# Eight K loads cut into 112 rows and four transfers of four rows, and seven 126-row dk stores moved to other heads

## The chip, the cores and the metric

One core of one Trainium2 chip. The metric is the device time of one execution in microseconds (us), as the median of several runs.

## The reference, cut to what matters

```python
B, H, Sq, Sk, D = 2, 32, 1, 8192, 128          # bf16
def fwd(q, k, v):
    scores = einsum("bhqd,bhkd->bhqk", q, k) * D ** -0.5
    return einsum("bhqk,bhkd->bhqd", softmax(scores), v)
# outputs: fwd, and its gradients dq, dk, dv for a given grad_out
```

There are 64 heads. Each reads a K and a V matrix of 8192 x 128 bf16 (2,048 KB each) and writes a dK and a dV of the same size. That is 537 MB in all, against little arithmetic, so the kernel is a stream.

## The kernel before

A K or V matrix lies in SBUF as a tile of 128 partitions with 64 x 128 bf16 each: a *row* of 16 KB per partition. There are twelve such tiles. VectorE overwrites K and V with dK and dV, and the tile is stored and then filled again, six heads later. Loads are issued by SyncE (queue q1 of the profile), stores by GpSimd (q0). Both queues are served by the same 16 DMA engines: in the trace of the kernel before, the longest unbroken chain of packets, each starting 3 or 4 ns before the end of the last (426 packets, from 87 to 312 us), holds load rows of q1 and store rows of q0, in turn at 87% of its steps.

```python
SPREAD = range(5, 64, 9)
...
def by_rows(eng, dst, src, rows):
    p = 0
    for m in rows:
        pin(eng.dma_start(out=dst[p : p + m], in_=src[p : p + m], max_dma_last_dim=NT * D))
        p += m

def load(i, w, pieces=(NCH,)):                 # w = 0: K, w = 1: V
    h = heads[i]
    t = kvp.tile([P, NT, D], BF16, tag=f"kv{slot_of(i, w)}", name="kvt")
    h.tile[w] = t
    src = (v_v if w else k_v)[i]
    c = 0
    for m in pieces:
        n0, n1 = c * CH, (c + m) * CH
        pin(load_eng.dma_start(out=t[:, n0:n1, :], in_=src[:, n0:n1, :]))
        c += m
...
def outer(i, w, c, ends):                      # dK (w = 0) or dV, into the tile, and its store
    ...
    if w == 0 and i in SPREAD:
        by_rows(store_eng, dst, h.tile[w], (P - 2, 2))
    else:
        eng = load_eng if len(ends) > 1 else store_eng
        pin(eng.dma_start(out=dst[:, b0:b1, :], in_=h.tile[w][:, b0:b1, :]))
```

A normal load is one transfer of 128 rows, eight for each engine (eight 16 KB packets for each load in that chain). The dk stores of the seven heads in `SPREAD` go as 126 rows and 2 rows. The chain has 18 packets of 8 KB, or nine rows, of such a store, so 126 rows fill 14 engines, and most of the work is kept off the other two (4 and 5 by the prediction's reading of the trace). No profile shows an engine's number: the numbers in this document are my names for chains of packets.

## Time and profile before

| | before |
|---|---|
| time, median of 3 runs | 1288.12 us (1287.0 to 1288.25) |
| moved by DMA | 539.68 MB |
| TensorE busy | 88% of the span |
| ScalarE, VectorE busy | 76%, 73% |
| DMA busy | 90% or more in 39 of 40 slices |

The profile page of the kernel before opens with the span and the busy time of each engine (us, share, instructions), and further down counts the DMA packets:

```profile
span 1286.9 us, 42575 instructions
...
PE 1131.8 (88%) x19268; PEld 860.1 (67%) x19268; DVE 935.9 (73%) x2122; ACT 975.2 (76%) x641; POOL 75.1 (6%) x142
...
DMA packets 39986, 539.68 MB, mean 419 GB/s; under 512 B 5116, under 2 KB 5116, under 8 KB 6396
```

No compute engine is full over the whole run. 539.68 MB at a mean of 419 GB/s is the time. The prediction shows the DMA, queue and chain lines; they say that the DMA engines are the bound. This stretch of the middle of the kernel before (columns: stretch and length, busy us and instructions of TensorE, weight load, VectorE, ScalarE and GpSimd, TensorE clock, DMA share, GB/s) is the mark to compare with later:

```profile
120.00:160.00 40.00, 39.36 (x704) 30.41 (x703) 33.51 (x76) 35.40 (x24) 3.54 (x6) 1.00 1.01 427
```

In this early stretch TensorE is nearly full as well (39.36 of 40 us). Over the run it is not: it is 88% busy, and 91.6 us of the rest are waits for loads (below).

### The profile page before, as it was taken

How to read it: one execution, taken by the hardware profiler on the slowest of the kernel's cores; microseconds unless marked ns; L12 is line 12 of the kernel's file. 1: busy time of each engine (PE TensorE's matmuls, PEld its weight loads, DVE VectorE, ACT ScalarE, POOL GpSimd, SP SyncE). 2: the span in 40 equal slices, each digit the busy share in tenths (PEclk: the TensorE clock that was granted, in tenths of full speed). 3: DMA queues.
4: the chain of work that ended last, by engine and by line, in shares of the span. 5: the costliest groups of instructions: out<-in, count | busy, mean ns of one | idle time of the engine just before them, and what ended most of it. 6: DMA issues, size and time to landing. Idle time of an engine off the chain costs nothing.

```text
span 1286.9 us, 42575 instructions
## 1 busy us (share of the span) xinstructions
PE 1131.8 (88%) x19268; PEld 860.1 (67%) x19268; DVE 935.9 (73%) x2122; ACT 975.2 (76%) x641; POOL 75.1 (6%) x142
## 2 busy tenths in 40 slices
PE   6999999988899988989899988889898988988880
PEld 5777777766677666766666766667666666766650
DVE  2888888777687777767776876777767777777781
ACT  6888888877788777867777877778777777777750
POOL 0000000000000000000000000000000000000000
PEclk9999999999899999989899998999999999999985
DMA  9999999999999999999999999999999999999995
GB/s 388 424 425 427 427 427 427 426 427 428 428 426 427 428 427 426 416 429 427 427 427 429 427 427 427 427 424 424 426 427 428 426 427 424 427 428 428 424 392 216
DMA packets 39986, 539.68 MB, mean 419 GB/s; under 512 B 5116, under 2 KB 5116, under 8 KB 6396
## 3 DMA queue, kind: packets, MB, share of 16 engines
q1 hardware_dynamic: 20172, 272.70, 49.8%
q0 software_dynamic: 19632, 264.25, 48.7%
q8 instruction: 150, 2.46, 0.7%
q14 instruction: 32, 0.26, 0.0%
HBM read 268.47 MB, written 268.47 MB: 417 GB/s over the span
## 4 chain that ended last, share of the span: by engine, by line
DMA 38%; PE 26%; another core or an unknown queue 19%; DVE 10%; issue 4%; ACT 1%; SPq 1%; POOL 0%; POOLq 0%; DVEq 0%; ACTq 0%
DMA kvt<-in_v_dram 29%; PE tp L184 11%; PE acc L339 6%; DVE kvt L394 6%; DMA kvt<-in_k_dram 5%; DMA out_dram<-kvt 4%; PE dpw L195 3%; PE sw L195 3%; DVE sel L362 2%; ACT ev L186 1%; PE dpw L282 1%; SPq L98 1%; DVE sel L356 1%; DMA qd_nat<-in_q_dram 1%
## 5 line engine op out<-in xcount | busy, mean ns | idle before, releaser
L186 ACT COPY ev<-tp 128x2048 bf16<-128x2048 bf16 x512 | 954.4, 1865 | 266.1 <-PE tp L184 254.4
L184 PE MATMUL tp<-ident_bf,kvt 128*128 128x128 bf16 x8192 | 559.9, 223 | 91.6 <-DMA kvt<-in_v_dram 71.6
L394 DVE TENSOR_TENSOR kvt<-qb,pair 128x2048 bf16<-128x2048 bf16 x512 | 621.4, 1214 | 0.3
L184 PEld LDWEIGHTS <-kvt 128*128 128x128 bf16 x8192 | 490.5, 101 | 98.3 <-DMA kvt<-in_v_dram 75.1
L195 PEld LDWEIGHTS <-ev 128*128 128x128 bf16 x8192 | 243.1, 96 | 210.0 <-issue 152.5
L339 PE MATMUL acc<-kvt,dS_pad 128*64 128x512 bf16 x1024 | 169.2, 413 | 0.8 <-DVE dqT L379 0.8
L339 PE MATMUL acc<-kvt,E_pad 128*64 128x512 bf16 x1024 | 161.0, 395 | 0.0
L195 PE MATMUL dpw<-qdT,ev 128*128 128x1 bf16 x4096 | 140.8, 164 | 17.7 <-DVE qb L177 16.9
L362 DVE SCALAR_TENSOR_TENSOR sel<-acc,diag,sel 128x128 f32<-128x128 f32 x384 | 134.7, 351 | 13.6
L195 PE MATMUL sw<-qdT,ev 128*128 128x1 bf16 x4096 | 142.0, 164 | 1.2 <-ACT ev L186 1.2
L412 POOL DMA_DIRECT2D out_dram<-kvt x119 | 63.7, 536 | 1087.6 <-DVE kvt L394 922.1
L207 DVE TENSOR_REDUCE mp<-sw 128x1 f32<-128x64 f32 x64 | 14.4, 224 | 151.8 <-PE sw L195 151.8
L339 PEld LDWEIGHTS <-dS_pad 128*64 128x64 bf16 x1024 | 37.7, 111 | 24.7 <-issue 5.9
L247 DVE CAST E_pad<-E_f 128x64 bf16<-128x64 f32 x64 | 12.5, 195 | 55.4 <-ACT E_f L238 55.4
L339 PEld LDWEIGHTS <-E_pad 128*64 128x64 bf16 x1024 | 36.5, 109 | 21.4 <-issue 0.9
L376 PE MATMUL acc<-ones,sel 128*128 128x1 f32 x256 | 43.6, 239 | 6.2 <-DVE sel L362 6.2
L282 PE MATMUL dpw<-ld,ones 128*128 128x1 f32 x256 | 46.3, 250 | 0.1
L253 DVE CUSTOM_DVE_ANT_0 junk<-E_f,dpw 128x64 bf16<-128x64 f32 x64 | 14.1, 221 | 43.7 <-PE dpw L195 43.7
L376 PEld LDWEIGHTS acc<-ones,sel 128*128 128x128 f32 x256 | 39.3, 194 | 7.3 <-DVE sel L362 7.3
L356 DVE TENSOR_SCALAR sel<-acc,diag 128x128 f32<-128x128 f32 x128 | 44.1, 344 | 0.0
L177 DVE CAST qb<-dpw 128x128 bf16<-128x128 f32 x128 | 35.5, 277 | 6.2 <-PE dpw L168 6.2
L282 PEld LDWEIGHTS dpw<-ld,ones 128*128 128x128 f32 x256 | 38.2, 189 | 0.5 <-DVE ld L253 0.5
(44 smaller groups left out, 313.2 us busy)
## 6 DMA issues: line engine op xcount, KB each, us to landing
out_dram<-kvt POOLq DMA_DIRECT2D x119, 2048.0 KB, 66.9
kvt<-in_v_dram SPq DMA_DIRECT2D x64, 2048.0 KB, 20.9
kvt<-in_k_dram SPq DMA_DIRECT2D x63, 2048.0 KB, 20.9
out_dram<-kvt POOLq DMA_DIRECT2D x7, 2016.0 KB, 70.3
out_dram<-kvt SPq DMA_DIRECT2D x8, 512.0 KB, 24.0
kvt<-in_k_dram SPq DMA_DIRECT2D x2, 512.0 KB, 4.7
kvt<-in_k_dram SPq DMA_DIRECT2D x1, 1024.0 KB, 7.3
out_dram<-kvt POOLq DMA_DIRECT2D x7, 32.0 KB, 69.7
```

What stands on the lines that cost most here:

```text
L177: pin(nc.vector.tensor_copy(out=h.qb[w][:], in_=h.qbp))
L184: pin(nc.tensor.transpose(tp[:, t, :], src[:, c * CH + t, :], ident_bf[:]))
L186: pin(nc.scalar.copy(out=ev[:], in_=tp[:]))
L195: nc.tensor.matmul(dst[:, c * CH + t : c * CH + t + 1], lhsT=ev[:, t, :], rhs=qdT[:, w, i : i + 1], start=True, stop=True,)
L207: pin(nc.vector.reduce_max(out=h.mp[:], in_=h.s, axis=AX.X))
L282: nc.tensor.matmul(out, lhsT=ones[:].to_broadcast([P, P]), rhs=col, start=True, stop=True)
L339: nc.tensor.matmul(h.acc[w][g : g + CW, :], lhsT=wts[:, n0 : n0 + CW], rhs=rows[:, n0 : n0 + QT, :].rearrange("p n d -> p (n d)"), start=( ...
L356: nc.vector.tensor_scalar(out=h.sel[:], in0=block, scalar1=diag[:, 0:1], scalar2=None, op0=ALU.mult)
L362: nc.vector.scalar_tensor_tensor(out=h.sel[:], in0=block, scalar=diag[:, b : b + 1], in1=h.sel[:], op0=ALU.mult, op1=ALU.add,)
L376: nc.tensor.matmul(h.acc[w][:, 0:1], lhsT=h.sel[:], rhs=ones[:], start=True, stop=True)
L394: nc.vector.tensor_tensor(out=h.tile[w][:, n0 : n0 + CH, :].rearrange("p n (e t) -> p n e t", t=2), in0=h.qb[w][:] .rearrange("p (e t) -> ...
L412: pin(eng.dma_start(out=dst[:, b0:b1, :], in_=h.tile[w][:, b0:b1, :]))
```

## The change

Intent: engines 0 to 3 seemed to have less work than the others at the end of the kernel. In eight K loads, the change moves one row from each of engines 4 to 15 to engines 0 to 3: 112 rows over all 16 engines (seven each), then four transfers of four rows, each on four engines. The step of 4 in the row index picks, for each small transfer, rows that lie four partitions apart. The seven dk stores without engines 4 and 5 come every eight heads from head 4, in place of every nine from head 5.

```diff
-SPREAD = range(5, 64, 9)
+EXTRA = range(8, 64, 7)
+SPREAD = range(4, 56, 8)
...
         src = (v_v if w else k_v)[i]
+        if w == 0 and i in EXTRA:
+            m = P - 16
+            pin(load_eng.dma_start(out=t[:m], in_=src[:m]))
+            for j in range(4):
+                r = slice(m + j, P, 4)
+                pin(load_eng.dma_start(out=t[r], in_=src[r], max_dma_last_dim=NT * D))
+            return
         c = 0
```

## The prediction

14.6 us for 24 rows and 0.3 us for their small packets make 14.9, and 1,288.1 + 14.9 = 1,303, taken as 1,302.5. That engines 0 to 3 get 7 + 4 rows was an assumption.

> **What bounds the kernel now.** I read the page's forty slices first, then the queues, the chain of work that ended last, the DMA issues, the stretches of the last 67 us, and at last the single DMA packets.
>
> ```profile
> DMA  9999999999999999999999999999999999999995
> GB/s 388 424 425 427 427 427 427 426 427 428 428 426 427 428 427 426 416 429 427 427 427 429 427 427 427 427 424 424 426 427 428 426 427 424 427 428 428 424 392 216
> q1 hardware_dynamic: 20172, 272.70, 49.8%
> q0 software_dynamic: 19632, 264.25, 48.7%
> q8 instruction: 150, 2.46, 0.7%
> q14 instruction: 32, 0.26, 0.0%
> DMA 38%; PE 26%; another core or an unknown queue 19%; DVE 10%; issue 4%; ACT 1%; SPq 1%; POOL 0%; POOLq 0%; DVEq 0%; ACTq 0%
> out_dram<-kvt POOLq DMA_DIRECT2D x119, 2048.0 KB, 66.9
> kvt<-in_k_dram SPq DMA_DIRECT2D x63, 2048.0 KB, 20.9
> out_dram<-kvt POOLq DMA_DIRECT2D x7, 2016.0 KB, 70.3
> ```
>
> The 16 DMA engines are busy in every slice but the last, at some 427 GB/s. Loads (q1) and stores (q0) share them about evenly. A store needs 66.9 us to land while a head (two loads, two stores) takes about 1,287/64 = 20 us, so some six or seven stores always stand in line. TensorE is 88% busy, with waits for loads in it. The DMA engines are the bound, and what remains is how evenly they are loaded. The last 27 us show that they are not even:
>
> ```profile
> 1220.00:1240.00 20.00, 18.56 (x333) 14.45 (x332) 15.32 (x38) 16.35 (x13) 1.06 (x2) 1.00 1.00 402
> 1240.00:1260.00 20.00, 11.37 (x82) 5.55 (x80) 17.34 (x36) 1.86 (x1) 0.53 (x1) 0.60 0.96 393
> 1260.00:1287.00 27.00, 0.00 (x0) 0.00 (x0) 0.00 (x0) 0.00 (x0) 0.00 (x0) 0.50 0.43 177
> ```
>
> These are stretches with the busy time of TensorE, its weight load, VectorE, ScalarE and GpSimd; the last three numbers are TensorE's clock, the share of DMA busy and GB/s. From 1,260 us on no compute is left and the DMA engines are busy to 0.43: fewer than half work, the others have nothing left. So the span is set by the engines with most work; the mean hides it.
>
> **The engines one by one.** The packet records carry no engine number, but an engine's packets follow one another exactly. A 16 KB packet takes 611 ns, and the next of its engine starts 3 or 4 ns before its end. I followed these links, with the fixed pattern of each engine (8 rows and one 4-byte completion per transfer, load and store rows in turn), from the start to the end. This gives 16 chains. Two checks: the 150 packets of q8 fall on eight chains, in a rotation that never breaks; and in the seven 126-row stores exactly two chains get the two spare rows (four 8 KB packets are two rows). Identity comes from the start: the 58-row q load put 29 packets of 256 B on each of two chains (engines 0 and 1), and the six rows that Pool loads fell on these two and four more (0 to 5), among which are the two of the spare rows (4 and 5). Position of each chain at 1,229 us, in 16 KB rows behind the freest one, and its last packet (us from the span's start; a few chains cross in the tail, so its ends are good to some 4 us):
>
> ```
> one of 0,1    19 instruction fetches        43 behind   1284.8
> other of 0,1  9 gaps of 0.3 us (q14)        13          1265
> one of 2,3    none                           6          1260
> other of 2,3  17 gaps of 0.3 us (q14)       28          1274
> 4 and 5       one with fetches, one slowed  52, 85 (49 of them planned)   1260, 1273
> six of 6-15   19 or 18 fetches each         39 to 42    1280 to 1282
> four of 6-15  none                           0 to 10    1260 to 1265
> ```
>
> A fetch costs its engine its own 986 ns and about 407 ns of stretch in the next packet: about 1.38 us. 19 of them are 26 us, or 43 rows of 0.607 us: just the lag seen. One of the engines 4 and 5 has 1,742 stretched packets, 53 us in all, and the present stores without 4 and 5 (7 x 7 rows less on each) repay it.
>
> [...] 58 rows came on two engines, 29 each, and 126 on 14. [...] the chains show load and store rows alternating. [...] The trace has the 16 KB packets, but on a saturated engine their 1.38 us are not hidden.
>
> **The change part by part.**
>
> *K loads.* Each of the eight heads (8, 15, ... 57) moves one row from each of engines 4 to 15 to engines 0 to 3, which get 7 + 4 = 11 rows in place of 8. In sum engines 0 to 3 get 8 x 3 = 24 rows more, 24 x 0.607 = 14.6 us; engines 4 to 15 get 8 rows less, 4.9 us. The four-row transfers are cut in 8 KB packets (309 ns in the trace, two of them 610 against 607 ns for a row): 32 rows x 3 ns and 32 completions of some 6 ns are 0.3 us more. SyncE issues 32 more transfers of about 0.33 us each, beside idle time. The instruction order shows each waiting only for loads of three or four transfers before, which have landed by then: nothing.
>
> *dk stores.* Still seven, from head 4 every eighth instead of from 5 every ninth. Same rows for each engine, earlier by up to seven heads: no time.
>
> *Compute.* The same instructions in the same order on TensorE, VectorE and ScalarE: no time of its own.
>
> *Sum.* New last packets: the engine of 0 and 1 with the fetches, 1,284.8 + 14.6 + 0.3 = 1,299.7 us; the other of them about 1,280; engines 2 and 3 about 1,275 and 1,289; the fetching engines of 6 to 15, 1,281 - 4.9 = about 1,277. The last engine is the one that the change loads. The span keeps its 2 us after the last packet, so it grows by about 14.9 us: 1,288.1 + 14.9 = 1,303. I take 1,302.5, a little less, for the chance that a part is absorbed.
>
> **The rivals.**
>
> 1. *The intended gain.* If engines 0 to 3 were all light, the ends would come together: the fetching ones fall by 4.9 us, and the kernel ends near 1,283. For it: half of the engines are idle in the tail, and three of the four receivers are lighter than the latest. Against: the fetching one among 0 and 1 already ends last, and even without it the q14 engine would reach 1,289 and cancel the gain. The identity rests on one trace; if the fetches sit on other engines in another run, this rival holds, with 1,283 to 1,292.
>
> 2. *Hidden.* The stores in line (six or seven) absorb an uneven load for a while, and the landing of K is hidden by six heads of prefetch: 1,288. Against: lag is never given back, it grew linearly (the fetching chains 6, 13, 20, 27, 34, 41 rows behind at 200, 400, ... 1,200 us). It is a backlog that must be drained at the end.
>
> 3. *Amplified.* The lag of the worst engine against the freest grows from 43 to 43 + 24 + 8 = 75 rows, over four stores. Then buffers come free later, the free engines may run dry in the middle, and an irregular K load (11 rows on four engines, landing perhaps 6 us later) may hold TensorE and delay the tail. It would take the time to 1,308 or more. Against: the worst engine itself always has work in line, so its own sum sets the end.
>
> **Range and chances.** The sum is 1,303 if the fetch engines stay where they are, which I give four chances in five; the rest spreads over 1,283 to 1,298. Rival 3 adds a few us above. So 1,290 to 1,308 holds it 8 times in 10. Slower by over 2% means over 1,313.9 and needs rival 3 in full: 5%. Faster by over 2% means under 1,262.4, just what the freest engines reach (1,260 and the 2 us): 1%.
>
> **What will show it.** Right: the last 27 us of the changed kernel have a longer thin end in which only a few engines work; the page's mean GB/s falls to about 414 with the same bytes; followed packet by packet, one of the two chains with 29 packets of 256 B at the start carries 24 rows more and ends last, at about 1,300, and the other fetching chains end some 20 us before it. The issue list has eight K loads of 1,792 KB and 32 of 64 KB. Wrong: the fetches lie on other chains than in the kernel before; or the chains end together; or the DMA row shows idle slices in the middle (rival 3); or the four-row transfers spread over engines other than 0 to 3.

## The result, and the profile after

The changed kernel takes **1308.74 us** (1307.73 to 1311.37, 4 runs), against 1288.18 us (1287.0 to 1289.45, 4 runs) of the kernel before in the same rounds. The ratio is 1.0163, with a 95% interval of 1.0144 to 1.0181. Ratios here are the mean time of one kernel's fast runs over that of the other's fast runs of the same rounds, so not quite the ratio of the medians. It is slower by 20.6 us: within 2%, but 0.7 us above the predicted range, and 5.7 us more of a loss than the 14.9 us that were worked out.

The page of the changed kernel, with the lines that answer to those of before:

```profile
span 1307.6 us, 42655 instructions
...
PE 1130.6 (86%) x19268; PEld 860.3 (66%) x19268; DVE 936.4 (72%) x2122; ACT 975.8 (75%) x641; POOL 75.3 (6%) x142
...
DMA  9999999999999999999999999999999999999985
GB/s 389 423 426 413 394 427 429 423 398 427 428 428 404 426 422 426 417 424 422 423 425 417 427 425 423 413 429 428 421 406 424 423 428 396 407 420 427 423 359 220
DMA packets 40242, 539.68 MB, mean 413 GB/s; under 512 B 5244, under 2 KB 5244, under 8 KB 6524
...
q1 hardware_dynamic: 20428, 272.70, 49.8%
q0 software_dynamic: 19632, 264.25, 48.4%
...
DMA 47%; issue 16%; PE 16%; another core or an unknown queue 10%; DVE 7%; SPq 1%; POOL 1%; ACT 1%; POOLq 0%; DVEq 0%; ACTq 0%
```

The bytes are the same, and so is the compute, to 1.2 us per engine. The DMA row is full as before. What is new is in the GB/s row: about every four slices it dips, to 394, 398, 404, 417 and so on. A slice is 32.7 us wide, the eight K loads are seven heads or some 140 us apart, and the dips keep that beat. In those slices the engines are as busy as ever and move less.

This can be added up from the page alone. Take 428 GB/s as full speed. A slice at g GB/s has lost (428 - g)/428 of its width. Over slices 2 to 38 that is 4.5 us before and 22.5 us after, 18.0 us more; over the last two slices (the tail) 18.6 and 21.2, 2.5 us more. Together this is 20.5 us of the 20.7 us by which the two spans differ. So **nearly all of the loss happens in the middle, at the changed loads**, and not at the end, where the prediction put it.

The same stretch as above, now around the first cut load, and the tail:

```profile
120.00:160.00 40.00, 39.19 (x690) 29.77 (x687) 33.39 (x75) 35.17 (x24) 2.73 (x5) 1.00 1.01 390
```

```profile
1220.00:1240.00 20.00, 18.60 (x301) 13.98 (x301) 14.57 (x33) 15.02 (x11) 1.07 (x2) 0.91 1.01 428
1240.00:1260.00 20.00, 17.45 (x304) 13.33 (x305) 15.10 (x37) 15.81 (x11) 1.07 (x2) 1.00 0.88 370
1260.00:1287.00 27.00, 22.17 (x345) 15.51 (x343) 21.98 (x49) 15.30 (x11) 1.60 (x3) 0.94 0.70 294
1287.00:1308.00 21.00, 3.91 (x16) 1.80 (x14) 8.45 (x17) 0.00 (x0) 0.00 (x0) 0.50 0.53 210
```

In the first fence the DMA share is 1.01, as before, and 390 GB/s stand where 427 stood. In the second, the compute of the last heads lies some 37 us later than before (VectorE starts its last work on a K or V tile at 1,292.5 us in place of 1,255.0), and the end is thin as it was.

What was foretold of the cut itself did come. The list of DMA issues of the changed kernel (KB of one transfer, and us from issue to landing where the view gives it):

```profile
out_dram<-kvt POOLq DMA_DIRECT2D x119, 2048.0 KB, 50.0
...
kvt<-in_k_dram SPq DMA_DIRECT2D x8, 1792.0 KB
...
kvt<-in_k_dram SPq DMA_DIRECT2D x32, 64.0 KB
```

Who waits for loads is seen in the list of waits (the waiting engine and line, what it waited for, total us, times, longest). Before and after:

```profile
PE tp L184 <- DMA kvt<-in_v_dram: 71.6, 41, 4.7
PE tp L184 <- DMA kvt<-in_k_dram: 20.0, 26, 2.0
```

```profile
PE tp L192 <- DMA kvt<-in_k_dram: 70.7, 34, 10.8
PE tp L192 <- DMA kvt<-in_v_dram: 50.0, 33, 3.6
```

TensorE's waits for loads grow from 91.6 to 120.7 us, and K takes the place of V in them: single waits now last up to 10.8 us. These waits show where the loads are late, not what the late loads cost: the experiment e4 below waits longer for K, and takes no more time than the kernel before.

**Packet by packet.** The records of single DMA packets give the size of it. I took the usual duration of each size of packet from the kernel before (611 ns for 16 KB, 309 for 8 KB, 159 for 4 KB). For the sizes that only e4 and e8 have I took 535 ns for 14 KB, and 81 for 2 KB (their median is 84, so 3 us of e4's stretch below are of this choice). All time above the usual I call *stretch*. Every instant of every engine is then rows at usual speed, stretch, instruction fetches, or idle. Divided by 16 engines, in us:

| | packets' span | rows | stretch | fetches | idle |
|---|---|---|---|---|---|
| before | 1285.4 | 1245.8 | 12.4 | 9.8 | 17.4 |
| after | 1304.3 | 1245.9 | 29.1 | 10.1 | 19.2 |

Of 18.9 us, 16.7 are stretch. (The spans of the two executions differ by 20.7 us; the other 1.8 us lie outside the packets, at the ends.) In the first cut load the packets of the 112-row transfer took 812 ns on average, in the later ones 660 to 743, in place of 611. Stores that ran beside the first took 686, other loads 733, and over the run the stretch of stores rose from 141 to 248 us of engine time. The 8 KB pieces of the four-row transfers kept their 309 ns. From 50 to 950 us all engines together were idle for less than 1.5 us in either kernel, so nothing starved in the middle.

### The profile page after: what moved, and what is told of

Read it like the earlier page. It is cut to its first block, busy times and chain, and to the rows that moved or that the text cites. A ratio compares the mean times of both kernels' runs of the same rounds, so it can differ in the third digit from the quotient of the medians.

```text
span 1307.6 us, 42655 instructions
## 1 busy us (share of the span) xinstructions
PE 1130.6 (86%) x19268; PEld 860.3 (66%) x19268; DVE 936.4 (72%) x2122; ACT 975.8 (75%) x641; POOL 75.3 (6%) x142
## 2 busy tenths in 40 slices
DMA packets 40242, 539.68 MB, mean 413 GB/s; under 512 B 5244, under 2 KB 5244, under 8 KB 6524
## 4 chain that ended last, share of the span: by engine, by line
DMA 47%; issue 16%; PE 16%; another core or an unknown queue 10%; DVE 7%; SPq 1%; POOL 1%; ACT 1%; POOLq 0%; DVEq 0%; ACTq 0%
DMA kvt<-in_v_dram 19%; DMA kvt<-in_k_dram 16%; DMA out_dram<-kvt 11%; PE tp L192 7%; DVE kvt L402 4%; PE acc L347 4%; PE sw L203 2%; PE dpw L203 2%; DVE sel L370 1%; ACT ev L194 1%; POOL out_dram L420 1%; SPq L101 1%; DMA qd_nat<-in_q_dram 1%; PE dpw L290 0%
## 5 line engine op out<-in xcount | busy, mean ns | idle before, releaser
L192 PE MATMUL tp<-ident_bf,kvt 128*128 128x128 bf16 x8192 | 560.2, 223 | 127.3 <-DMA kvt<-in_k_dram 70.7
L347 PE MATMUL acc<-kvt,dS_pad 128*64 128x512 bf16 x1024 | 164.3, 403 | 1.9 <-DVE dqT L387 1.9
L347 PE MATMUL acc<-kvt,E_pad 128*64 128x512 bf16 x1024 | 163.7, 401 | 0.0
```

The lines of the kernel that those rows point to most:

```text
L192: pin(nc.tensor.transpose(tp[:, t, :], src[:, c * CH + t, :], ident_bf[:]))
L347: nc.tensor.matmul(h.acc[w][g : g + CW, :], lhsT=wts[:, n0 : n0 + CW], rhs=rows[:, n0 : n0 + QT, :].rearrange("p n d -> p (n d)"), start=( ...
```

## The experiments

Fifteen kernels were run. Three theories stood at the start. *Sum*: the extra rows land on the engine that ends last (the prediction). *Shape*: a K load that isn't one transfer of 128 rows moves slowly. *Moved stores*: the dk stores at other heads cost it. The second was later split in two: is it the row count, or the partitions that the rows go to? I guessed that a row is slow if another engine brings it to its partition than does so in a 128-row load; that was not shown. No profile shows an engine's number beside a partition, so which engine fills which partition is not known here. What could be tested by the times is whether the partitions of a transfer matter.

How the rows of a transfer fall on engines was read from chains of packets (8 of 128 rows on each of 16 chains, 7 of 112, 9 of 126 on 14, and by the prediction 29 of 58 on two). Where no trace is named, the row counts of the experiments were chosen on the assumption that other counts are dealt out evenly as well.

In the measurements, "stretch" is the total over all engines, in us of engine time (before: 198; after: 466). Divided by 16 it compares with the time.

### Each part alone: e1, e2

e1 is the kernel before with the stores of the change; e2 is the changed kernel with the stores of before.

```diff
# e1, against before            # e2, against after
-SPREAD = range(5, 64, 9)       -SPREAD = range(4, 56, 8)
+SPREAD = range(4, 56, 8)       +SPREAD = range(5, 64, 9)
```

> The kernel before with only the dk-store part of the change (heads 4, 12, ... 52). Theory (the 112-row loads stretch packets, the stores are innocent): 1288, within 3 us of the kernel before, stretch of the packets as before (about 198 us of engine time in the whole run). Rival (moving the stores costs part of the 20 us): 1292 or more.

Measured: 1284.52 us, ratio 0.9975 (0.9959 to 0.9992); stretch 172.

> The changed kernel with the dk stores at the old heads (5, 14, ... 59): only the K loads differ from the kernel before. Theory: all of the loss is here, 1305 to 1311, stretch about 466 us of engine time. Rival (the loss needs the stores to meet the K loads): below 1298.

Measured: 1303.82 us, ratio 1.0124 (1.0109 to 1.0139); stretch 434.

The stores alone gain 3.6 us, against "no time" in the prediction. The K loads alone cost 15.7 us. The sum is 12.1, and the whole change costs 20.6: the two parts don't add up (see e12). Of the gain of e1, (198 - 172)/16 = 1.6 us is stretch; the rest was not taken apart. The seven 126-row stores are the only irregular transfers of e1, and their 8 KB packets took 315 ns on average against the usual 309.

### Shape or amount: e3, e4

e3 keeps the 112-row transfer but is meant to spread the other 16 rows over all engines, so that no engine gets more bytes than before. e4 does the reverse: it is meant to give engines 0 to 3 the same extra bytes as the change, but by columns. Seven eighths of every row go by a transfer of 128 partitions, and the last eighth of rows 0 to 123 and 124 to 127 by two transfers; four chains of its trace are marked by them.

```diff
# e3
+            pin(load_eng.dma_start(out=t[:m], in_=src[:m]))        # m = 112
+            pin(load_eng.dma_start(out=t[m:], in_=src[m:], max_dma_last_dim=NT * D))
# e4
+            n0 = NT - NT // 8
+            pin(load_eng.dma_start(out=t[:, :n0, :], in_=src[:, :n0, :]))
+            for r in (slice(0, P - 4), slice(P - 4, P)):
+                pin(load_eng.dma_start(out=t[r, n0:, :], in_=src[r, n0:, :]))
```

> The kernel before with the eight K loads as 112 rows on all engines plus one transfer of 16 rows, also on all 16: each engine has the 8 rows that it had before, nothing goes to engines 0 to 3. Theory (the shape itself stretches packets[...]): still 1300 to 1312, 112-row packets at about 700 to 800 ns in the first such load against 611. Rival A (the 24 extra rows on engines 0 to 3 set the end, as predicted): 1288, within 3 us. Rival B (the late landing of K's last rows on engines 0 to 3): 1288 to 1292.

Measured: 1301.55 us, ratio 1.0106 (1.009 to 1.0123); stretch 398.

> The same bytes moved to engines 0 to 3 as in the change (each 4 rows' worth more and one less per load: 11 against 7), but the shape kept: 128 rows of 14 KB on 16 engines, and the last 2 KB of each row as 124 rows plus 4 rows on engines 0 to 3. Theory: no stretch (about 200 us), the time from the engines' sums alone: the engine of 2 and 3 with the gaps of q14 ends near 1289 and the fetching ones near 1280, so 1288 to 1293. Rival A (the extra rows on engines 0 to 3): 1303. Rival B (K lands late on four engines): 1300 or more.

Measured: 1288.12 us, ratio 1.0004 (0.9989 to 1.0019); stretch 252. The GB/s row of e4 has no beat of dips:

```profile
GB/s 387 427 426 426 423 427 428 428 425 427 427 427 427 429 427 423 423 428 428 425 429 415 422 421 428 426 426 411 426 428 426 424 421 423 425 428 416 426 383 286
```

The loss formula of above gives 8.6 us for slices 2 to 38 of e4 and 14.1 for its tail (before: 4.5 and 18.6). So the end did become more even, as the change intended, and the middle took the gain back. The waits for K are longer than in the changed kernel, at no cost in time:

```profile
PE tp L191 <- DMA kvt<-in_k_dram: 79.7, 18, 14.5
```

So the bytes on engines 0 to 3, the whole subject of the prediction's sum, cost nothing on balance, a late K does not set the time either, and the shape alone, meant to be without any extra bytes, costs 13.4 of the 15.7 us. *Sum* has fallen.

### Which shapes: e5, e6, e7

e5 loads the eight K tiles as rows 0 to 63 and 64 to 127; e6 as 126 rows and 2; e7 cuts five loads into odd counts, to number the engines in the trace.

```diff
# e5
+            for r in (slice(0, P // 2), slice(P // 2, P)):
+                pin(load_eng.dma_start(out=t[r], in_=src[r]))
# e6: the same with (slice(0, P - 2), slice(P - 2, P))
# e7: 96 + 12 + 10 + 8 + 2 rows in head 9, 96 + 14 + 13 + 5 in head 12, and so on
```

> The kernel before with the eight K loads as two halves of 64 rows, each on 16 engines: every engine has its 8 rows as before, the packets are 16 KB, 64 is a power of two, and no transfer is small. [...] Theory[...]: 1325 to 1370. Rival A (112 rows are slow because 7 rows per engine are odd, or because of the many small transfers): 1288, within 3 us.

Measured: 1305.62 us (1299.49 to 1316.3), ratio 1.0138 (1.0074 to 1.0201); stretch 414. A loss, but of 16.5 us, less than half of the least that was expected (1325). If all the added stretch is that of these loads, it is (414 - 198)/1,024 = 0.21 us for each of their packets. The four runs scatter by 16.8 us, so the size is rough.

> The kernel before with the eight K loads as 126 rows (14 engines[...]) and 2 rows (engines 0 and 1). [...] Theory[...]: packets of these loads near 611 to 640 ns, stretch in the whole run below 260 us of engine time against 198 before and 434 with 112 rows; the time by sums, with one row more on most engines in each of eight loads (4.9 us on the fetching ones): 1288 to 1295. Rival (any shape but 128 rows is slow): packets of 700 ns or more and 1300 or more.

Measured: 1309.96 us, ratio 1.0158 (1.0132 to 1.0184); stretch 476, the worst of the three. The theory expected hardly any loss here (stretch below 260, 1288 to 1295), and fell in that form. What was left was: the loss depends on the partitions that a transfer fills. A rival was left as well: anything but one transfer of 128 rows is slow, for a reason that has nothing to do with partitions.

> The kernel before, with five K loads (heads 9, 12, 15, 18, 21) cut into transfers of 96 rows and of 16, 15, 14 ... 2 rows[...]. It tells where the instruction fetches are. The prediction: one of engines 0 and 1 has fetches. The changed kernel's trace says instead: none of 0 to 3; one of 4 and 5, seven of 6 to 15. [...] Time of no interest, some 1290 to 1305.

Measured: 1303.93 us, one run of unknown state. As a numbering it is inconclusive: packets of the cut loads stretched (462 in all), the links between an engine's packets broke at the first of them, and not every engine could be named.

### Other addresses in the device memory: e11

e11 loads each of the eight K tiles by one 128-row transfer again, from every second row of two heads. Its output is wrong, which doesn't matter for the time.

```diff
+    k_far = (k.rearrange("b h s d -> (b h s) d")
+             .rearrange("(g p two n) d -> g p two n d", p=P, two=2, n=NT))[:, :, 0]
...
+            pin(load_eng.dma_start(out=t[:], in_=k_far[i // 2]))
```

> The eight K loads as one 128-row transfer as in the kernel before, but from every second 16 KB row of two heads, so that the pattern in HBM changes and the SBUF side does not (wrong result on purpose). Theory[...]: 1288, within 3 us, stretch about 200. Rival (HBM side: what matters is which rows the engines read together): 1292 or more, stretch above 260.

Measured: 1287.61 us, ratio 1.0007 (0.9987 to 1.0027); stretch 197. Other addresses in the device memory, same partitions: no loss. This was tried for one other pattern, in 128-row transfers only.

### The halves exchanged: e9, e10

Both load eight K tiles as one 64-row transfer and eight transfers of eight rows, each on eight engines only (the page of e10 counts 5,628 packets under 512 B, 512 more than before for 64 such transfers, eight for each). In e9 the small ones are rows 0 to 63; in e10 the halves are exchanged, and the small ones are rows 64 to 127.

```diff
# e9, in place of the change's five transfers; e10 has own, rest = 64, 0
+            own, rest = 0, 64
+            pin(load_eng.dma_start(out=t[rest : rest + 64], in_=src[rest : rest + 64]))
+            for p in (own, own + 32):
+                for j in range(4):
+                    r = slice(p + j, p + 32, 4)
+                    pin(load_eng.dma_start(out=t[r], in_=src[r]))
```

> The eight K loads as one transfer of rows 64 to 127 (16 engines) and eight transfers of 8 rows with step 4 for rows 0 to 63, which go to engines 0 to 7[...]. To be compared with the next run, which has the same counts, sizes and engines. Theory[...]: stretch of all packets 260 to 330 us of engine time (198 before, 414 with both halves as 64-row transfers). Rival (HBM side, or the shape itself): the same stretch as in the next run, within 40 us. Engines 0 to 7 have 12 rows per load in both: 1295 to 1310.

Measured: 1309.13 us, ratio 1.0175 (1.0152 to 1.0198); stretch 337.

> As the run before with the halves exchanged: the eight transfers of 8 rows, still on engines 0 to 7, fill partitions 64 to 127[...]; rows 0 to 63 are the one 64-row transfer. Theory:[...] stretch 400 to 520 us of engine time, at least 100 us more than in the run before, and 5 us or more longer. Rival (HBM side, or the shape itself): the same as the run before.

Measured: 1330.69 us, ratio 1.0335 (1.032 to 1.0351); stretch 523.

The same transfers and bytes, and 21.6 us between them; 186/16 = 11.6 us of that is stretch and 10.9 us idle (37.6 against 26.7 us per engine). This speaks for partitions. But both kernels load their engines unevenly, as the idle time shows, and e9 loses 1.75% itself, so it doesn't say that any of these transfers is free. In both kernels, engines also ran dry in the middle, which those of the changed kernel hardly did.

### The two parts together: e12

e12 is the changed kernel with the dk stores every seven heads from head 7, so that they don't meet the K loads.

```diff
-SPREAD = range(4, 56, 8)
+SPREAD = range(7, 56, 7)
```

> The changed kernel with its seven 126-row dk stores at heads 7, 14, ... 49, so that each is executed between two of the 112-row K loads; in the changed kernel the first and the last of these loads meet such a store (packets stretched by 62 and 76 us of engine time there, against 39 and 33 with the stores at the old heads). Theory (the two parts of the change do not add up[...]): first and last load about 30 to 45 us of stretch each, 400 to 440 in the whole run, 1298 to 1304. Rival (no interplay): 1307 to 1311, as the changed kernel.

Measured: 1305.04 us, ratio 1.0127 (1.011 to 1.0144); stretch 417. In the changed kernel the first and the last cut load had 62 and 76 us of stretch around them, the six between 23 to 45; they are the two that run beside a 126-row store. In e12 these two have 38 and 31. The time was 1 us above what was expected. The meeting is worth about 3.7 us (1308.7 to 1305.0). The rest of the 8.5 us by which the parts fail to add up stays open; part of it is idle time (307 us of engine time after, 247 in e2).

### The same transfer, moved by 32 partitions: e13, e14, e15

The last question was whether partitions or the mere shape make the loss. All three kernels load K whole, as before, and then 64 of its rows a second time, with the same data, behind the head's V load. Only the first row differs (in the tile, and with it in the device memory).

```diff
+EXTRA = range(8, 64, 7)
+FROM = 32                       # e14: 0, e15: 64
...
+        if w == 1 and i in EXTRA:
+            r = slice(FROM, FROM + 64)
+            pin(load_eng.dma_start(out=h.tile[0][r], in_=k_v[i][r]))
```

> The kernel before, whose eight K tiles of the change are loaded whole by one 128-row transfer as before, and then rows 32 to 95 of them once more, same data, by one 64-row transfer behind the head's V load: four rows to each of 16 engines. [...] Bytes: 8 x 4 rows x 0.611 us = 19.6 us more for every engine, so about 1,307.7 us without any stretch. Theory[...]: 1,306 to 1,310, packets stretched by 170 to 240 us of engine time in all, as before (198). Rival (any load that isn't 128 rows is slow, whatever its partitions): stretch about 340, as in the run with 64 + 8 x 8 rows, 1,314 to 1,322, and the same as the next run.

Measured: 1306.05 us (1305.4 to 1307.21), ratio 1.0135 (1.011 to 1.016); stretch **187**.

> As the run before in every transfer, wait and byte, but the rows loaded twice are 0 to 63[...]. Theory: stretch of some 300 to 350 us of engine time and 1,312 to 1,322 us, at least 5 us above the run before. Rival: the same as the run before within 2 us.

Measured: 1319.33 us (1317.14 to 1325.49), ratio 1.0231 (1.0199 to 1.0263); stretch **455**.

> As the two runs before, rows 64 to 127 twice[...]. Theory: as rows 0 to 63, 1,312 to 1,322 us, stretch 300 to 350. Rival: all three the same within 2 us.

Measured: 1324.42 us (1321.15 to 1326.76), ratio 1.0275 (1.0242 to 1.0307); stretch **432**.

The extra bytes are 8 x 4 rows x 0.611 = 19.6 us for each engine, and the table of rows gives 1265.3 us for all three, 19.5 more than before. e13 pays just these (17.8 us, with a little less idle). e14 and e15 pay 13.3 and 18.4 us more, for the same transfers and bytes. In the executions that were profiled (1307.21, 1325.49 and 1322.22 us) it is 18.3 and 15.0 us, and their stretch, divided by 16, is 16.8 and 15.3 us above that of e13. The page shows it without any table. The GB/s rows of e13, e14 and e15, and the landing of the K transfers of 1,024 KB (eight of the nine are the second loads):

```profile
GB/s 389 422 428 427 427 428 426 427 428 428 425 429 427 427 428 427 425 430 429 424 429 423 424 427 428 426 427 427 426 428 428 427 425 426 428 428 428 421 355 257
...
kvt<-in_k_dram SPq DMA_DIRECT2D x9, 1024.0 KB, 14.9
```

```profile
GB/s 390 425 426 428 383 428 426 427 404 427 425 428 422 412 425 427 427 412 427 428 426 400 427 426 429 427 401 424 417 427 412 427 412 425 416 426 426 421 375 223
...
kvt<-in_k_dram SPq DMA_DIRECT2D x9, 1024.0 KB, 16.3
```

```profile
GB/s 391 423 428 427 384 425 429 426 402 428 426 427 417 412 425 427 428 403 427 427 428 394 428 427 427 420 420 425 428 426 413 427 421 425 416 422 429 425 353 266
...
kvt<-in_k_dram SPq DMA_DIRECT2D x9, 1024.0 KB, 16.3
```

In e13 the row is flat at its second loads. In e14 and e15 it dips to 383 and 384 at the first of them, as in the changed kernel. The loss formula of above gives 3.7 us for slices 2 to 38 of e13, 20.1 for e14 and 18.8 for e15 (before 4.5, after 22.5). A 64-row load from partition 32 costs its bytes and no more; **the same load from partition 0 or 64 costs 13 to 18 us more**. The rival of e6 has fallen.

Three limits remain. With the partitions, the rows that are read from the device memory move too; e11 speaks against these, but no run holds them fixed. And not every load of few rows is slow: the 256 packets of the four-row transfers in the changed kernel took 310 ns on average, against the usual 309. The loss is shown for loads of 64 to 126 rows. And that the 112-row loads are slow for the same reason is carried over from e13 to e15; they were not moved by themselves.

Why such loads are slow was not measured: no run shows what the engines share. Nor do the losses simply add: e5 loads rows 0 to 63 and rows 64 to 127 of its eight tiles and lost 16.5 us, while the same two loads in e14 and e15 cost 13.3 and 18.4 us more than that of e13. What makes up the difference was not taken apart.

### A version that beats both: e8

e8 takes the stores of the change, and the columns of e4 in every second of its heads.

```diff
-SPREAD = range(5, 64, 9)
+EXTRA = range(8, 64, 14)
+SPREAD = range(4, 56, 8)
...                              # the load of e4
```

> The dk stores at heads 4, 12, ... 52 (1284.5 alone) with the column form of the K loads at four heads (8, 22, 36, 50): engines 0 to 3 get 12 rows' worth more, the others 4 less (2.4 us). Theory (sums set the tail, column form costs little): 1281 to 1285. Rival (the column form costs as much as it balances, as at eight heads): 1285 to 1288.

Measured: 1283.15 us (1281.89 to 1284.49), ratio 0.9956 (0.9938 to 0.9975); stretch 202, idle 9.3 us per engine against 17.4. It is the fastest kernel, 25 us below the changed one. Most of its gain is that of e1 (1284.52); the 1.4 us between them lie within the intervals, so what the columns add is not shown.

## Why the prediction was right or wrong

- **What bounds the kernel**: right. Same compute, same bytes, and the time follows the DMA engines alone.
- **The cut**: right. Eight transfers of 1,792 KB and 32 of 64 KB, and exactly four chains of packets carry the 8 KB pieces. The mean fell to 413 GB/s, with 414 foretold.
- **"The last engine is the one that the change loads"**: this step failed. In the changed kernel's trace none of the four chains with the 8 KB pieces has an instruction fetch, and neither do the four marked chains of e4 and e8. So the chain with 19 fetches, which ended last, is not one of engines 0 to 3. In the trace of before, as I read it now, two chains cross at the start, with packet ends 1 ns apart; I took the wrong pairing, and put the fetches on one of 0 and 1. With the right one, the prediction's own sums become its rival 1, 1,283 to 1,292. e4, which moves the same bytes without the shape, gave 1288.12: no loss where the sum had 14.9 us.
- **A row is 0.607 us**: this is the term that was missing. The sum took rows of the 112-row transfer at the usual speed. They took 812 ns in the first cut load and 660 to 743 in the later ones, and slowed stores and loads beside them. This is 16.7 us per engine in the table above, and most of the 20.6 us. That the 14.9 us of the sum came near the measured 15.7 of e2 is chance: e3, meant to have no extra row on engines 0 to 3, loses 13.4.
- **dk stores, "no time"**: wrong by 3.6 us of gain when alone (e1), and some 3.7 us of loss where a store meets a cut load (e12).
- **Rival 2, hidden**: K's landing was not wholly hidden (TensorE's waits for K rose from 20.0 to 70.7 us), but waits are not what set the time.
- **Rival 3, amplified**: its number, 1,308 or more, came true, its mechanism didn't. Engines hardly ran dry before about 950 us, and idle time grew by 1.8 us per engine only. Here the engines stay busy and lose speed, which no rival contained.
- **Range**: the upper edge was missed by 0.7 us. The 5% of "slower by over 2%" was not needed.

## What to carry to other kernels

In this stream a load as one transfer of 128 rows kept its speed, also from other addresses (e11, 1287.61 us), and single engines could be given more bytes by cutting columns at no cost in time (e4, 1288.12). Row counts that merely divide by 16 cost 13.4 us (112 and 16, e3) and 16.5 us (64 and 64, e5). Where a part of a tile has to be loaded, measure its first partition too: from 32 it cost its bytes alone, from 0 or 64 it did not (stretch 187 against 455 and 432). When a DMA-bound kernel slows down with the same bytes, look at the GB/s row under a full DMA row first, and only then at the order of engines at the end. A sum over engines is only as good as the duration of each packet in the new shape, and that can be had from one run of the shape alone.
